# Head 1's first loads on ScalarE's queue, head 0's first key cast on GpSimd, in a fused block-sparse attention and gated MLP kernel

## The chip, the core and the metric

The kernel runs on one core of one Trainium2 chip. The core has four engines that compute: TensorE (PE in the profile, with its weight loads as PEld), VectorE (DVE), ScalarE (ACT) and GpSimd (POOL). SyncE (SP) only issues DMAs here. SP and ACT each have a DMA queue of their own, which the page lists as q1 (SP) and q10 (ACT). The metric is the device time of one launch in microseconds (us). The kernel before was timed three times: the median is 210.89 us, the lowest 209.82, the highest 212.28.

## The reference

Attention over 4 batches, 8 heads, 768 positions, 64 dimensions per head, in fp32, followed by a gated MLP with a spatial mixing step. In short:

```
scores = q @ k.T / sqrt(64)
allowed = |block_i - block_j| <= 1, or block 0 or 23 on either side,
          or block_j among the 3 sampled blocks of block_i    # blocks of 32
attn = softmax(where(allowed, scores, -1e9)) @ v
x = heads side by side                       # [4, 768, 512]
h = relu(x @ w_in)                           # 1024 wide
u, v = halves of h;  v = (v - mean(v)) / sqrt(var(v) + 1e-6)
v = w_spatial @ v + b_spatial                # over the 768 positions
out = (u * v) @ w_out                        # [4, 768, 512]
```

## The kernel before

**Tiling.** Two heads of one batch make a pair, so there are 16 pairs, four to a batch. Keys, queries and values of a pair are loaded as fp32 with the positions over 128 partitions and six chunks per partition (`load`, tiles `st_k`, `st_q`, `st_v`), cast to bf16 (`cast`, tile `nat` for keys and queries, `vv` for values), and transposed so that the head's 64 dimensions lie on partitions (tile `kq`). Under those 64 rows `kq` has 24 more: for the keys the one-hot of the key's block, for the queries a penalty of -300 per block that is not allowed. One matmul with 88 rows thus gives masked scores.

**Slots.** The main loop runs in slots. In each slot TensorE makes a tile of scores in PSUM (L443 in the first batch, L456 later), ScalarE takes the exponential of it into `a_all` (L448, L460), and some slots later TensorE multiplies it by the values (L489, L507). There are two score tiles (tag `sc`), so TensorE can be at most two slots ahead of ScalarE. The first batch takes 36 slots, cut into thirds of the queries so that work can begin before everything is loaded; pair 0, which comes first, is cut by head: slots 0 to 2 are head 0, slots 3 to 5 head 1. Steps of the MLP are dealt out between the slots by tables written by hand (`STEPS`, `AV_AT`, `ROWS`, `when(...)`).

**Order.** The order on every engine is the order of the program text (`manual_schedule`); each engine and each queue takes its instructions strictly in that order and waits where an instruction's input is not there. What is touched here is the start:

- The mask's one-hot and penalty rows are made from `sampled_blocks` (tile `samp`) by GpSimd and VectorE. TensorE turns the penalty into the mask rows of `kq` (L296), and ScalarE copies two of the three results out of PSUM (L222).
- ScalarE first issues the loads of head 0's keys (chunks 0 to 3, then 4 and 5). Then comes a dummy exponential on the tile `tiny` (L163), ahead of which the activation table is loaded, then the cast of head 0's first keys (L136), then the copies out of PSUM, and from then on the exponentials.
- SyncE issues `samp`, head 0's first queries, head 1's keys, head 1's first queries, and then the loads of the other pairs in the order written: keys, first queries of pair 1, values of pair 0, keys of pair 3, keys of pair 2, and so on, later the first weights of the MLP (`w_f`, L229). `st_k` has three buffers: the load of pair 2's keys is the fourth, and takes the buffer of pair 0.
- GpSimd casts head 0's first queries (L138), head 0's last keys, head 1's keys, copies mask rows (L249), casts head 1's first queries, and then the casts of the other pairs and of the weights in the order in which they are loaded.
- TensorE transposes head 0's keys and queries as they are cast (`head`, L303), and VectorE and ScalarE copy them into `kq` (`split0`, L219 and L222). Head 1 follows in `third()`, which runs behind slot 1's scores on TensorE and ahead of slot 2's. Its bank holds both the keys and the first queries.
- The second thirds of the queries of pairs 1, 2 and 3 are transposed in `tr_rest` at slots 12, 15 and 18 (L290), behind their cast on GpSimd.

Of the kernel before, what the change touches and what calls it, by code (L numbers as in the profile page):

```python
# [17 lines left out]
def _listify(ap: bass.AP) -> bass.AP:  # L18
    t = ap.tensor
    if isinstance(t.shape, tuple):  # L20
        t = dataclasses.replace(t, shape=list(t.shape))
        ap = dataclasses.replace(ap, tensor=t)
    return ap
# [3 lines left out]
def kernel(  # L27
# [16 lines left out]
    nc = tc.nc  # L44
# [50 lines left out]
    def dram(src, p, hs=slice(0, 2), cs=slice(0, NCH)):  # L95
        b, g = divmod(p, NG)
        return src[b, 2 * g + hs.start:2 * g + hs.stop].rearrange(
            "h (p c) d -> p h (c d)", c=NCH)[:, :, cs.start * D:cs.stop * D]

    H0, H1, BOTH = slice(0, 1), slice(1, 2), slice(0, 2)  # L100
    ALLC, C01, C03, C45 = slice(0, NCH), slice(0, TC), slice(0, 2 * TC), slice(2 * TC, NCH)
# [3 lines left out]
    def load(p, nm, hs=BOTH, cs=ALLC, eng=nc.sync):  # L105
        if (nm, p) not in st:
            st[nm, p] = work.tile([128, 2, S // 2], FP32, tag="gt" if (nm, p) == ("v", 0) else "st_" + nm,
                                   bufs=1 if (nm, p) == ("v", 0) else 4 if nm == "q" else 3,
                                   name="st_" + nm)
        eng.dma_start(out=st[nm, p][:, hs, cs.start * D:cs.stop * D],  # L110
                      in_=dram(SRC[nm], p, hs, cs))
# [4 lines left out]
    def nat0_view():  # L116
        return nat[0].rearrange("p c h d -> p (c h d)").rearrange("p (h x) -> p h x", h=2)

    def cast(p, nm, eng, hs=BOTH, cs=ALLC):
        if nm == "v":  # L120
            dst = vv[p % NVV][:, hs, cs, 0:D]
        else:
            if p not in nat:
                nat[p] = work.tile([128, 2 * NCH, 2, D], BF16, tag="nat", bufs=4, name="nat")
            c0 = 0 if nm == "k" else NCH
            dst = nat[p][:, c0 + cs.start:c0 + cs.stop].rearrange("p c h d -> p h c d")[:, hs]
        src = st[nm, p].rearrange("p h (c d) -> p h c d", d=D)[:, hs, cs]
        if p == 0 and nm != "v":
            dst = nat0_view()[:, hs, (c0 + cs.start) * D:(c0 + cs.stop) * D]
            if cs is not C45:  # L130
                dst = dst[:, 0].rearrange("p (i t d) -> p t i d", t=2, d=D)
                src = src[:, 0].rearrange("p (t i) d -> p t i d", t=2)
            else:
                dst = dst.rearrange("p h (c d) -> p h c d", d=D)
        if eng is nc.scalar:
            nc.scalar.activation(out=dst, in_=src, func=AF.Copy)  # L136
        else:
            eng.tensor_copy(out=dst, in_=src)  # L138

    samp = const.tile([KR, 2 * NR], I32)  # L140
    load(0,"k",H0,C03,eng=nc.scalar)
    load(0,"k",H0,C45,eng=nc.scalar)
    nc.sync.dma_start(out=samp[MR], in_=_listify(sampled_blocks).bitcast(I32))
    load(0,"q",H0,C03)
    load(0,"k",H1)
    load(0,"q",H1,C03)


    eq = const.tile([KR, NR + 1, NB], FP32)
# [66 lines left out]
    PL, DV = nc.gpsimd, nc.vector  # L216
# [31 lines left out]
        else:  # L248
            eng.tensor_copy(out=kq[MR, hs, cs], in_=src)  # L249

    cast(0, "k", nc.scalar, H0, C03)
    cast(0, "q", PL, H0, C03)
    rows(H1, K_)
    load(1, "k")
# [638 lines left out]
```

## Time and profile before

| what | value |
|---|---|
| median of three runs | 210.89 us (209.82 to 212.28) |
| profiled execution | 210.49 us, of which 208.7 us are the span shown |
| PE busy | 201.2 us (96%) |
| ACT busy | 167.6 us (80%) |
| DVE busy | 132.5 us (63%) |
| POOL busy | 71.2 us (34%) |
| data moved by DMA | 41.82 MB, of which SP's queue 40.91 MB and ACT's queue 0.59 MB |

The span begins with the first instruction that the profiler shows and ends with the last; the profiled execution is 1.79 us longer than its span. A time in a row of the timeline is counted from the start of the span. In a row of the timeline the first number is the start, the second how long it took from the first to the last of the merged instructions, then come the engine, the line, the operation, the tile written and the tile read, the shapes, and how many instructions were merged; in brackets stands the idle time of the engine just before, and what ended it.

### The profile page before, as it was taken

The page shows a single profiled execution, that of the slowest core. Times are in us where ns is not written, and L with a number is a line of the kernel's source. Part 1 is how long each engine was busy: PE and PEld are TensorE (multiplying, and loading weights), DVE is VectorE, ACT ScalarE, POOL GpSimd, SP SyncE. Part 2 cuts the span into 40 slices and gives each one's busy share as a digit, 9 for nine tenths or more (in the row PEclk, how much of TensorE's full clock was granted, in tenths as well). Part 3 has the DMA queues.
Part 4 walks back from the last instruction along what each step waited for, and adds up shares of the span by engine and source line. Part 5 has one row for each costly group of instructions (what it writes and reads, how often), then busy time and mean ns, then how long its engine had stood idle before and what let it go on. Part 6 is the DMA issues. An engine that isn't in the chain of part 4 may idle for free.

```text
span 208.7 us, 5245 instructions
## 1 busy us (share of the span) xinstructions
PE 201.2 (96%) x2107; PEld 127.6 (61%) x2141; DVE 132.5 (63%) x294; ACT 167.6 (80%) x222; POOL 71.2 (34%) x110
## 2 busy tenths in 40 slices
PE   8899999999999999999999999999999999999993
PEld 6588878766666666655565555665556556544441
DVE  6999687878754545484986455376785433567542
ACT  5899899999989989989998888979999787266021
POOL 5588889566573314042065040131020000003000
PEclk9999999999999999999999999999999999999999
DMA  5999999999999999999735597793101324610266
GB/s 140 341 366 347 291 350 222 296 210 298 256 373 220 276 185 315 260 286 342 181 141 113 115 257 171 231 319 86 38 3 21 67 53 85 244 66 0 50 148 254
DMA packets 64139, 41.82 MB, mean 200 GB/s; under 512 B 45172, under 2 KB 58868, under 8 KB 64116
## 3 DMA queue, kind: packets, MB, share of 16 engines
q1 hardware_dynamic: 63540, 40.91, 75.2%
q10 hardware_dynamic: 576, 0.59, 0.9%
q8 instruction: 16, 0.26, 0.5%
q14 instruction: 7, 0.06, 0.1%
HBM read 24.38 MB, written 6.29 MB: 147 GB/s over the span
## 4 chain that ended last, share of the span: by engine, by line
PE 84%; DMA 7%; ACT 2%; issue 2%; SPq 1%; POOL 1%; DVE 1%; ACTq 0%; POOLq 0%
PE ps_moe L581 31%; PE ps L456 22%; PE ps_av L507 12%; PE ps_t L581 8%; PE ps L443 4%; DMA w_f<-in_moe_w_in_dram 4%; PE ps_sc L581 4%; DMA st_k<-in_k_dram 3%; PE ps_av L489 2%; SPq L110 1%; ACT a_all L448 1%; PE ps L290 1%; POOL w_in_t L235 1%; ACT osb L222 0%; PE ps_av L290 0%
## 5 line engine op out<-in xcount | busy, mean ns | idle before, releaser
L460 ACT ACTIVATE a_all<-ps 128x768 bf16<-128x768 f32 x144 | 113.4, 811 | 14.5 <-PE ps L456 8.3
L456 PE MATMUL ps<-kq 88*128 88x384 bf16 x288 | 70.4, 325 | 0.4
L507 PEld LDWEIGHTS <-a_all 128*128 128x128 bf16 x864 | 45.2, 97 | 20.0
L507 PE MATMUL ps_av<-vv,a_all 128*128 128x65 bf16 x864 | 49.8, 193 | 0.0
L456 PEld LDWEIGHTS <-kq 88*128 88x128 bf16 x288 | 27.7, 98 | 29.7
L581 PE MATMUL ps_moe<-w_in_t,xt 128*128 128x512 bf16 x127 | 38.6, 378 | 0.5
L448 ACT ACTIVATE a_all<-ps 128x1024 bf16<-128x1024 f32 x36 | 34.3, 1026 | 2.5 <-PE ps L443 2.0
L581 PE MATMUL ps_moe<-vn,w_spt 128*128 128x512 bf16 x99 | 30.2, 377 | 0.4
L138 POOL CAST nat<-st_k 128x768 bf16<-128x768 f32 (+2 forms) x17 | 13.4, 790 | 43.3 <-DMA st_k<-in_k_dram 41.6
L620 POOL TENSOR_SCALAR std<-mv 128x3 f32<-128x3 f32 (+1 forms) x9 | 2.1, 238 | 60.8 <-DVE mv L617 43.7
L443 PE MATMUL ps<-kq 88*128 88x256 bf16 (+1 forms) x140 | 21.6, 275 | 0.8 <-DVE kq L219 0.3
L653 DVE SCALAR_TENSOR_TENSOR un<-ps_moe,b_col,un 128x512 bf16<-128x512 f32 x18 | 13.4, 747 | 13.5 <-PE ps_moe L581 11.4
L471 DVE RECIPROCAL rc<-ps_av 128x6 f32<-128x6 f32 (+1 forms) x36 | 6.6, 185 | 23.4 <-PE ps_av L507 21.5
L581 PEld LDWEIGHTS <-xt 128*128 128x128 bf16 x192 | 15.5, 98 | 7.6 <-DVE xt L219 0.2
L581 PE MATMUL ps_moe<-w_out_t,gt 128*128 128x512 bf16 x66 | 19.6, 378 | 0.2
L472 DVE TENSOR_TENSOR xn<-ps_av,rc 128x384 bf16<-128x384 f32 (+1 forms) x36 | 18.5, 513 | 1.2
L616 DVE BATCH_NORM_STATS2 stats<-vn 128x6 f32<-128x512 bf16 x24 | 16.4, 684 | 1.3 <-ACT vn L611 0.9
L138 POOL CAST nat<-st_q 128x768 bf16<-128x768 f32 (+2 forms) x21 | 14.7, 705 | 5.9 <-DMA st_q<-in_q_dram 5.8
L219 DVE COPY kq<-tt 64x1536 bf16<-64x1536 bf16 x24 | 14.9, 620 | 1.8 <-DMA tt<-nat 1.5
L443 PEld LDWEIGHTS <-kq 88*128 88x128 bf16 x140 | 12.5, 97 | 4.6 <-DVE kq L219 0.9
L581 PEld LDWEIGHTS <-w_spt 128*128 128x128 bf16 x144 | 11.6, 98 | 5.6
L138 POOL CAST vv<-st_v 128x768 bf16<-128x768 f32 x15 | 13.0, 867 | 4.1 <-DMA st_v<-in_v_dram 2.7
(83 smaller groups left out, 206.1 us busy)
## 6 DMA issues: line engine op xcount, KB each, us to landing
st_v<-in_v_dram SPq DMA_DIRECT2D x16, 384.0 KB, 6.0
st_k<-in_k_dram SPq DMA_DIRECT2D x15, 384.0 KB, 4.6
out_dram<-osb SPq DMA_DIRECT2D x22, 256.0 KB, 2.9
st_q<-in_q_dram SPq DMA_DIRECT2D x12, 384.0 KB, 4.8
ws_f<-in_moe_w_spatial_dram SPq DMA_DIRECT2D x6, 384.0 KB, 9.1
w_f<-in_moe_w_in_dram SPq DMA_DIRECT2D x8, 256.0 KB, 5.9
w_f<-in_moe_w_out_dram SPq DMA_DIRECT2D x4, 256.0 KB, 4.1
st_q<-in_q_dram SPq DMA_DIRECT2D x6, 128.0 KB, 5.9
```

Source lines behind the costliest of these rows:

```text
L138: eng.tensor_copy(out=dst, in_=src)
L219: nc.vector.tensor_copy(out=o, in_=i)
L443: nc.tensor.matmul(out=ps[:, at:at + n * TW], lhsT=kq[:, h, ci * 128:(ci + 1) * 128], rhs=kq[:, h, qcols(t0, n)], start=True, stop=True)
L448: nc.scalar.activation(out=out, in_=ps, func=AF.Exp, scale=0.125)
L456: nc.tensor.matmul(out=ps[:, hf * 512:hf * 512 + HALF], lhsT=kq[:, j % H, ci * 128:(ci + 1) * 128], rhs=kq[:, j % H, S + hf * HALF:S + (hf ...
L460: nc.scalar.activation(out=a_ref["h", j][:, ci, :].rearrange("p (b c) -> p b c", b=2), in_=ps.rearrange("p (b c) -> p b c", b=2)[:, :, 0:H ...
L471: nc.vector.reciprocal(out=rc[:, 0:n], in_=ps[:, :, D:VA])
L472: nc.vector.tensor_tensor(out=out, in0=ps[:, :, 0:D], in1=rc[:, 0:n].to_broadcast([128, n, D]), op=ALU.mult)
L507: nc.tensor.matmul(out=av_ref[j][:, qc, 0:VA], lhsT=a_ref["h", j][:, ci, qc * 128:(qc + 1) * 128], rhs=vv[p % NVV][:, h, ci, 0:VA], start= ...
L581: nc.tensor.matmul(out=ref["ps"][:, 0:w], lhsT=lhs(i), rhs=rhs(i), start=(i == 0), stop=(i == n - 1))
L616: nc.vector.bn_stats(out=stats, in_=self.vn[:, tcc, :])
L653: nc.vector.scalar_tensor_tensor(out=self.un[:, tcc, :], in0=ps, scalar=b_col[:, tcc:tcc + 1], in1=self.un[:, tcc, :], op0=ALU.add, op1=AL ...
```

## The change

Two loads go from SyncE's queue to ScalarE's: all of head 1's keys in pair 0 (192 KB) and head 1's first queries (128 KB). They are issued behind the two loads that ScalarE already issued. And the cast of head 0's first keys, 128 partitions by 256 elements, goes from ScalarE to GpSimd, where it stands ahead of the cast of head 0's first queries.

```diff
     load(0,"k",H0,C03,eng=nc.scalar)
     load(0,"k",H0,C45,eng=nc.scalar)
+    load(0,"k",H1,eng=nc.scalar)
+    load(0,"q",H1,C03,eng=nc.scalar)
     nc.sync.dma_start(out=samp[MR], in_=_listify(sampled_blocks).bitcast(I32))
     load(0,"q",H0,C03)
-    load(0,"k",H1)
-    load(0,"q",H1,C03)
...
-    cast(0, "k", nc.scalar, H0, C03)
+    cast(0, "k", PL, H0, C03)
     cast(0, "q", PL, H0, C03)
     rows(H1, K_)
```

## The prediction

> **What bounds the kernel now.** I read the page first, then the waits of TensorE and ScalarE stretch by stretch, then the first 30 us of the timeline, engine by engine.
>
> ```profile
> PE 201.2 (96%) x2107; PEld 127.6 (61%) x2141; DVE 132.5 (63%) x294; ACT 167.6 (80%) x222; POOL 71.2 (34%) x110
> ```
>
> TensorE is the engine of the whole span, but the edit touches the first microseconds. The question is which engine sets the pace there, and how much of a shift at the start reaches the end. ScalarE's timeline up to 30 us:
>
> ```profile
> 0.72 0.88 ACTq L110 DMA_DIRECT2D st_k<-in_k_dram  x2
> 1.63 1.28 ACT L163 ACT_TABLE_LOAD   x1 [1.63 <-PEq L877]
> 2.93 0.20 ACT L163 ACTIVATE tiny<-tiny 128x1 f32<-128x1 f32 x1
> 3.04 0.40 ACT L136 ACTIVATE nat<-st_k 128x256 bf16<-128x256 f32 x1
> 4.29 0.37 ACT L222 ACTIVATE kq<-mq 24x256 bf16<-24x256 f32 x1 [0.86 <-PE mq L296]
> ...
> 6.03 15.48 ACT L448 ACTIVATE a_all<-ps 128x1024 bf16<-128x1024 f32 x16 [0.57 <-PE ps L443]
> 22.11 5.83 ACT L448 ACTIVATE a_all<-ps 128x1024 bf16<-128x1024 f32 x6 [0.60 <-PE ps L443]
> ```
>
> The reader is to see the two long rows. From 6.03 to 21.51 sixteen exponentials run without a gap, 15.48 / 16 = 0.97 us each. In that stretch ScalarE sets the pace: an input that comes earlier buys nothing, one that comes too late opens a gap. At 21.51 comes the first gap, 0.60 us. TensorE's timeline has the reason, and GpSimd's the reason behind that:
>
> ```profile
> 21.02 0.40 PE L290 MATMUL ps<-ident,nat 128*128 128x128 bf16 x4 [0.43 <-POOL nat L138]
> ```
>
> ```profile
> 3.77 0.40 POOL L138 CAST nat<-st_q 128x256 bf16<-128x256 f32 x1 [0.99 <-DMA st_q<-in_q_dram]
> 4.11 0.29 POOL L138 CAST nat<-st_k 128x128 bf16<-128x128 f32 x1
> 4.79 0.51 POOL L138 CAST nat<-st_k 128x384 bf16<-128x384 f32 x1 [0.39 <-DMA st_k<-in_k_dram]
> 5.36 0.82 POOL L249 COPY kq<-kq 24x768 bf16<-24x768 bf16 x1
> 6.25 0.49 POOL L138 CAST nat<-st_q 128x256 bf16<-128x256 f32 x1
> ...
> 16.82 0.61 POOL L138 CAST nat<-st_q 128x512 bf16<-128x512 f32 x1 [0.47 <-DMA st_q<-in_q_dram]
> 17.49 0.61 POOL L249 COPY kq<-kq 24x512 bf16<-24x512 bf16 x1
> 18.47 0.61 POOL L235 CAST w_in_t<-w_f 128x512 bf16<-128x512 f32 x1 [0.37 <-DMA w_f<-in_moe_w_in_dram]
> 19.03 0.82 POOL L138 CAST vv<-st_v 128x768 bf16<-128x768 f32 x1
> 19.80 0.61 POOL L235 CAST w_in_t<-w_f 128x512 bf16<-128x512 f32 x1
> 20.36 0.61 POOL L138 CAST nat<-st_q 128x512 bf16<-128x512 f32 x1
> ```
>
> The cast of pair 2's later queries, 20.36 to 20.97, ends TensorE's wait. GpSimd comes to it late because it stood 0.47 us at 16.82 and 0.37 us at 18.47 for transfers. So the gap hangs on DMA, through GpSimd. TensorE's waits from 22 us to the end come back as an empty list: from there it runs on its own order. What the change can win is therefore the gap and little more: 0.43 us on TensorE, 0.60 on ScalarE.
>
> Now DMA. The windows of one microsecond (last three numbers: granted clock, DMA share, GB/s) and SyncE's issues:
>
> ```profile
> 3.00:4.00 1.00, 1.00 (x10) 0.75 (x9) 0.85 (x5) 0.43 (x2) 0.23 (x1) 1.00 0.93 297
> 4.00:5.00 1.00, 1.00 (x7) 0.54 (x6) 0.25 (x1) 0.69 (x2) 0.61 (x3) 1.00 0.66 107
> 5.00:6.00 1.00, 0.97 (x10) 0.67 (x8) 0.90 (x3) 0.44 (x2) 0.94 (x2) 1.00 0.80 268
> 6.00:18.00 12.00, 11.10 (x159) 8.83 (x158) 11.21 (x26) 11.70 (x13) 8.55 (x20) 1.00 1.07 360
> ```
>
> ```profile
> 1.21 0.37 SPq L110 DMA_DIRECT2D st_q<-in_q_dram  x1
> 1.64 0.41 SPq L110 DMA_DIRECT2D st_k<-in_k_dram  x1
> 2.09 0.43 SPq L110 DMA_DIRECT2D st_q<-in_q_dram  x1
> 2.57 0.43 SPq L110 DMA_DIRECT2D st_k<-in_k_dram  x1
> 3.05 0.47 SPq L110 DMA_DIRECT2D st_q<-in_q_dram  x1
> ...
> 4.08 1.61 SPq L110 DMA_DIRECT2D st_k<-in_k_dram  x2
> ```
>
> From 6 to 18 us the engines are full at 360 GB/s. Before, there is a hole: 107 GB/s from 4 to 5, 268 from 5 to 6. Pair 0's 640 KB are through, and pair 1's keys, issued only at 2.57, have hardly begun. Against 297, the rate of the microsecond before, the hole is 190 + 29 = 219 KB, at 360 GB/s 0.61 us; against 360 it is 253 + 92 = 345 KB, 0.96 us.
>
> **The change, part by part.**
>
> *Two issues leave SyncE.* The rows at 1.64 and 2.09 go, and what follows comes 2.57 - 1.64 = 0.93 us earlier: pair 1's keys at 1.64, pair 3's keys at 3.15 in place of 4.08. There the lead ends. Pair 2's keys need the buffer that the cast of head 1's keys sets free, and SyncE waits for it:
>
> ```profile
> SPq L110 <- POOL nat L138: 0.5, 1, 0.5
> ```
>
> That cast ends at 4.79 + 0.51 = 5.30. With the lead SyncE stands there 1.4 us in place of 0.5, and pair 2's keys go out at the same time as before. But four transfers, pair 1's keys and queries, pair 0's values, pair 3's keys (384 + 128 + 384 + 384 = 1280 KB), are in flight 0.93 us sooner, enough for 3.6 us at 360 GB/s. So the hole fills, and the full stream that follows is early by the 0.61 to 0.93 us (the issues' lead is the upper bound). I take 0.7, nearer the lower bound, since the microsecond ahead of the hole ran at 297 and not at 360.
>
> *What the lead is worth.* GpSimd's 0.47 us wait at 16.82 goes, since the transfer comes 0.7 earlier; then the wait of 0.37 at 18.47 too, which with 0.7 earlier is still met. The cast at 20.36 thus starts 0.70 us earlier, at 19.66, bounds 0.61 and 0.84 (both waits, all there is). TensorE needed it 0.43 us before it came. Its wait goes, **-0.43 us**, and ScalarE's gap shrinks from 0.60 to 0.17. Late next is nothing on GpSimd's side but TensorE's own order, so the 0.43 stays to the end.
>
> *Two issues more on ScalarE.* One costs 0.88 / 2 = 0.44 us, two 0.88. The table load begins at 2.51 in place of 1.63, ends at 3.79, the dummy exponential at 4.0. The next work, the copy at 4.29, waits for TensorE: 0.29 us of cover are left. Cost 0. If the table load or the issues took longer, each 0.1 us above 0.29 would shift the first exponential by as much; the only table load in the trace is this one of 1.28.
>
> *The cast moves.* On ScalarE it could not stay without cost: it would start at 4.1 in place of 3.04. On GpSimd the nearest rows with 128x256 are 0.40 and 0.49 us. The keys land 2.2 us after their issue at 0.72, so at 2.92; GpSimd is then idle (0.99 us before 3.77). The cast ends at 3.32 to 3.41; now it ends at 3.44.
>
> ```profile
> st_k<-in_k_dram ACTq DMA_DIRECT2D x1, 128.0 KB, 2.2
> 3.86 0.34 PEld L296 LDWEIGHTS <-bm 24*128 24x128 bf16 x3 [0.20 <-DVE bm L187]
> ```
>
> TensorE's next step waits for the mask at 3.86 anyway, so up to 0.1 us earlier buys nothing. Even as long as a 128x768 cast (0.82) it would be done at 3.74, before the queries that GpSimd casts next at 3.77. Cost 0, from 0 to the 0.1 by which a late end would push that cast.
>
> *Head 0's queries in new company.* The first exponential hangs on them: landing 2.5 us after 1.21, cast at 3.77, transposes at 4.61, copy, scores, exponential at 6.03. The rows are that landing, TensorE's weight load for the transposes, and the landing of head 1's keys:
>
> ```profile
> DMA to landing us min/median/max: 2.5/2.5/2.5
> 4.61 0.13 PEld L303 LDWEIGHTS <-nat 128*128 128x128 bf16 x2 [0.41 <-POOL nat L138]
> st_k<-in_k_dram SPq DMA_DIRECT2D x1, 192.0 KB, 3.1
> ```
>
> Head 1's keys are issued at 1.60 on ScalarE in place of 1.64 on SyncE, so the bytes in flight are the same, but they no longer stand behind the queries in one queue. Bounds: 0.3 us earlier (a landing in 2.2, as for the 128 KB above), or 1.03 later (landing with head 1's keys at 1.64 + 3.1 = 4.74). If half the 128 KB goes at half of 297 GB/s, it is 64 / 297 = 0.2 later. I take 0.1, which ScalarE's remaining gap of 0.17 at 21.51 takes up. The Trainium skill, page "DMA: Bandwidth & Descriptors", section "Queues, rings and completion order", says that each DMA engine goes round-robin between the queues that have work; by that rule two queues get half each, and the sum would take the 0.2, which leaves the total within 0.03 us of where it is. No run here shows the shares.
>
> **Sum** against the profiled execution: 210.49 - 0.43 + 0 + 0 + 0 = 210.06 us. The median of the three runs lies 0.40 above that execution; for the median I give **210.5 us**.
>
> **Rivals.**
>
> *The lead is hidden (210.9).* The bytes are the same, and if the hole at 4 to 6 us comes from the transfers' start and not from late issues, it merely moves. For it: 2.2 to 2.5 us pass from an issue to a landing even of the first ones. Against it: pair 0's 640 KB and the hole fit the issue times. Then GpSimd's casts stay where they are: 0. The Trainium skill, same page, section "Issuing engines are not separate DMA queues", states that issuing from several engines saves only the time of the issuing sequencer. By that rule the gain is at most the 0.93 us of SyncE's two issues, and nothing if something else holds the stream.
>
> *Head 1 comes late (slower, 211.7).* Head 1's first queries now land at 2.09 + 3.8 = 5.89 and are cast at 6.25; behind the cast, in TensorE's order, stand slot 2's scores. The rows are the landing of head 1's first queries, those scores, and the landing of pair 1's keys:
>
> ```profile
> DMA to landing us min/median/max: 3.8/3.8/3.8
> 7.11 0.59 PE L443 MATMUL ps<-kq 88*128 88x512 bf16 x2
> DMA to landing us min/median/max: 5.6/5.6/5.6
> ```
>
> Slot 2's exponential starts at 6.03 + 2 x 0.97 = 7.97 and needs scores from 7.38 on; they run at 7.11, so there are 0.27 us, and the cast may start as late as 6.52. That is where this rival decides. If pair 1's keys, now 0.93 us earlier, press the small load back until it lands as those do now (2.57 + 5.6 = 8.17), the cast starts 1.65 us too late and ScalarE's row of sixteen tears. Against it: the load has ScalarE's queue nearly to itself. Between 0 and 1.65 I take half, 0.8: 210.9 + 0.8 = 211.7; upper end 212.5. With head 0's 1.03 on top it would be 213.6.
>
> *More than the gap (210.0).* If ScalarE's next gap (0.29 us at 28.24) closes too, 0.60 + 0.29 = 0.89 off: 210.0.
>
> ```profile
> 28.24 2.14 ACT L448 ACTIVATE a_all<-ps 128x1024 bf16<-128x1024 f32 x2 [0.29 <-PE ps L443]
> ```
>
> **How the numbers follow.** Forecast 0.45, hidden 0.22, head 1 late 0.20, more than the gap 0.08, something that I do not see 0.05. A change of 1%, 2.1 us, is about what a measurement of this kernel can tell from none: its three runs lie 1.07 below to 1.39 above the median. No case but the pile-up of delays reaches 1% by itself; the spread of the runs adds on both sides. Faster by over 1%: 0.05 from forecast and hidden, 0.03 from more than the gap, 0.02 unseen, 0.10. Slower: 0.10 from the upper half of head 1 late, 0.04 from the spread, 0.03 unseen, 0.17. Within 1%: 0.73. The range goes from 210.0 - 1.1 = 208.9 to the late case's upper end and a little of the spread, 212.7.
>
> **What would show it.** Right: pair 1's keys issued near 1.64; the window from 4 to 5 us near 300 GB/s; no wait of GpSimd at 16 to 18.5; the gap at 21.5 under 0.3; first exponential at 6.0 to 6.2. Wrong: the hole still there (hidden); head 1's query cast after 6.5 and a gap among the first sixteen exponentials (late); a copy at 4.29 that follows the dummy exponential without idle time (ScalarE's issues cost more than their cover).

## The result and the profile after

The changed kernel is slower: 212.88 us (median of six runs, 212.49 to 214.43) against 210.64 for the kernel before in the same comparison, a ratio of 1.012 with a 95% interval of 1.0086 to 1.0155. The profiled execution took 212.74 us; its span is 210.6 us, 1.9 more than before. The forecast was 210.5, no change.

The page's first part; the busy time of ScalarE is what it was, TensorE's is 2.2 us more:

```profile
PE 203.4 (97%) x2107; PEld 129.4 (61%) x2141; DVE 135.7 (64%) x294; ACT 167.6 (80%) x221; POOL 72.3 (34%) x111
```

ScalarE's timeline, the same stretch as in the prediction:

```profile
0.72 1.38 ACTq L110 DMA_DIRECT2D st_k<-in_k_dram  x3
2.12 0.49 ACTq L110 DMA_DIRECT2D st_q<-in_q_dram  x1
2.64 1.28 ACT L163 ACT_TABLE_LOAD   x1 [2.64 <-issue]
...
6.45 1.98 ACT L448 ACTIVATE a_all<-ps 128x1024 bf16<-128x1024 f32 x2 [0.99 <-PE ps L443]
9.60 1.02 ACT L448 ACTIVATE a_all<-ps 128x1024 bf16<-128x1024 f32 x1 [1.17 <-PE ps L443]
...
12.20 4.87 ACT L448 ACTIVATE a_all<-ps 128x1024 bf16<-128x1024 f32 x5 [0.26 <-PE ps L443]
17.44 12.37 ACT L448 ACTIVATE a_all<-ps 128x1024 bf16<-128x1024 f32 x13 [0.37 <-PE ps L443]
30.10 2.14 ACT L448 ACTIVATE a_all<-ps 128x1024 bf16<-128x1024 f32 x2 [0.29 <-PE ps L443]
```

The row of sixteen exponentials without a gap is torn. The third one starts at 9.60, where before it would be 6.03 + 2 x 0.97 = 7.97. The tenth starts at 17.44, before at 6.03 + 9 x 0.9675 = 14.74: 2.70 us are lost by then. The 0.60 us gap that stood at 21.51 is gone, and the 23rd exponential starts at 30.10 against 28.24: 1.86 us, about what the span is longer by. GpSimd's timeline shows where it begins:

```profile
2.97 0.40 POOL L138 CAST nat<-st_k 128x256 bf16<-128x256 f32 x1 [0.20 <-DMA st_k<-in_k_dram]
...
6.40 0.51 POOL L138 CAST nat<-st_k 128x384 bf16<-128x384 f32 x1 [2.01 <-DMA st_k<-in_k_dram]
...
7.86 0.40 POOL L138 CAST nat<-st_q 128x256 bf16<-128x256 f32 x1
...
19.43 0.62 POOL L138 CAST nat<-st_q 128x512 bf16<-128x512 f32 x1
```

The moved cast runs at 2.97 and harms nobody. But head 1's keys, the second row, are cast at 6.40, not at 4.79, after 2.01 us of waiting for their DMA. Head 1's queries follow at 7.86, not at 6.25. TensorE meets this in `third()`:

```profile
5.38 1.04 PE L443 MATMUL ps<-kq 88*128 88x256 bf16 x4
...
7.17 0.53 PE L303 MATMUL ps<-ident,nat 128*128 128x128 bf16 x3
8.32 0.40 PE L303 MATMUL ps<-ident,nat 128*128 128x128 bf16 x2 [0.62 <-POOL nat L138]
8.51 1.06 PE L443 MATMUL ps<-kq 88*128 88x512 bf16 x2
```

Slot 2's scores, behind head 1's queries in TensorE's order, run at 8.51 and not at 7.11. VectorE then copies head 1 out of PSUM. Its timeline before, and after:

```profile
6.51 1.97 DVE L219 COPY kq<-ps 64x128 bf16<-64x128 bf16 x6
8.51 1.18 DVE L249 COPY kq<-kq 24x512 bf16<-24x512 bf16 x2
...
10.31 1.41 DVE L219 COPY kq<-ps 64x1024 bf16<-64x1024 bf16 x2
```

```profile
6.56 0.47 DVE L219 COPY kq<-ps 64x128 bf16<-64x128 bf16 x2
8.75 1.36 DVE L219 COPY kq<-ps 64x384 bf16<-64x384 bf16 x4 [1.72 <-PE ps L303]
...
12.62 1.41 DVE L219 COPY kq<-ps 64x1024 bf16<-64x1024 bf16 x2 [0.64 <-PE ps L290]
```

VectorE stands for 1.72 us, and pair 1's copies (64x1024) come 2.31 us later than before. In the windows before, VectorE was busy 11.21 of the 12 us from 6 to 18 and had little slack in which to catch up; after, it is 9.13. But it is not alone in keeping the delay: just ahead of pair 1's copies it stands once more, 0.64 us, for TensorE's transposes. TensorE's timeline shows no wait between 8.32 and 16 us, and up to 12.4 us the score matmuls of one slot take 1.03 to 1.06 us. The windows after:

```profile
3.00:4.00 1.00, 1.00 (x10) 0.78 (x9) 0.86 (x5) 0.99 (x2) 0.65 (x2) 1.00 0.95 177
4.00:5.00 1.00, 1.00 (x7) 0.54 (x6) 0.25 (x1) 0.83 (x3) 0.39 (x2) 1.00 0.96 356
5.00:6.00 1.00, 1.00 (x9) 0.60 (x7) 0.90 (x3) 0.43 (x2) 0.00 (x0) 1.00 1.09 333
6.00:18.00 12.00, 11.12 (x128) 8.62 (x127) 9.13 (x20) 9.40 (x10) 10.40 (x23) 1.00 0.97 326
```

The hole from 4 to 6 us is filled, though from 3 to 4 us less moves than before, 177 GB/s for 297. Whose bytes filled it is in the DMA rows of the first 5 us, by queue (q1 is SyncE's, q10 ScalarE's), first before, then after, with the landings of head 1's keys and queries:

```profile
q1 hardware_dynamic: 475, 0.49, 39.3%
q10 hardware_dynamic: 288, 0.20, 14.7%
```

```profile
q1 hardware_dynamic: 396, 0.45, 34.6%
q10 hardware_dynamic: 411, 0.37, 23.1%
st_k<-in_k_dram ACTq DMA_DIRECT2D x1, 192.0 KB, 4.7
st_q<-in_q_dram ACTq DMA_DIRECT2D x1, 128.0 KB, 5.1
```

Before, SyncE's 0.49 MB are all that head 0's queries and head 1's two loads hold (448 KB, 0.46 MB), with 0.03 MB left for pair 1. After, of head 1's 0.33 MB only about 0.37 - 0.20 = 0.17 have moved by 5 us, while SyncE's queue, less head 0's queries (0.13), has moved 0.32 MB of the loads behind them, which are cast from 8.51 us on. Head 1's keys land 4.7 us after their issue, before 3.1; the queries 5.1, before 3.8.

### The profile page after: what moved, and what is told of

It reads as the page before. It is cut to its first block, busy times and chain, and to the rows that moved or that the text cites. A ratio compares the mean times of both kernels' runs of the same rounds, so it can differ in the third digit from the quotient of the medians.

```text
span 210.6 us, 5244 instructions
## 1 busy us (share of the span) xinstructions
PE 203.4 (97%) x2107; PEld 129.4 (61%) x2141; DVE 135.7 (64%) x294; ACT 167.6 (80%) x221; POOL 72.3 (34%) x111
## 4 chain that ended last, share of the span: by engine, by line
PE 90%; issue 3%; ACT 2%; DVE 2%; POOL 1%; DMA 1%; SPq 0%; ACTq 0%; POOLq 0%
PE ps_moe L581 31%; PE ps L456 23%; PE ps_av L507 12%; PE ps_t L581 8%; PE ps L443 7%; PE ps_sc L581 4%; PE ps_av L489 3%; PE ps L290 1%; ACT a_all L448 1%; DMA st_q<-in_q_dram 1%; DVE kq L219 1%; POOL nat L138 1%; PE ps_av L290 0%; ACT osb L222 0%; ACT a_all L460 0%
## 5 line engine op out<-in xcount | busy, mean ns | idle before, releaser
L456 PEld LDWEIGHTS <-kq 88*128 88x128 bf16 x288 | 27.7, 98 | 29.7
L138 POOL CAST nat<-st_k 128x768 bf16<-128x768 f32 (+3 forms) x18 | 13.7, 759 | 40.3 <-DMA st_k<-in_k_dram 40.2
L443 PE MATMUL ps<-kq 88*128 88x256 bf16 (+1 forms) x140 | 24.0, 297 | 0.6 <-DVE kq L219 0.3
L219 DVE COPY kq<-tt 64x1536 bf16<-64x1536 bf16 x24 | 17.6, 733 | 0.3
L138 POOL CAST nat<-st_q 128x768 bf16<-128x768 f32 (+2 forms) x21 | 15.6, 743 | 5.9 <-DMA st_q<-in_q_dram 5.6
L443 PEld LDWEIGHTS <-kq 88*128 88x128 bf16 x140 | 13.3, 103 | 4.6 <-DVE kq L219 0.8
```

The lines of the kernel that those rows point to most:

```text
L219: nc.vector.tensor_copy(out=o, in_=i)
L443: nc.tensor.matmul(out=ps[:, at:at + n * TW], lhsT=kq[:, h, ci * 128:(ci + 1) * 128], rhs=kq[:, h, qcols(t0, n)], start=True, stop=True)
L456: nc.tensor.matmul(out=ps[:, hf * 512:hf * 512 + HALF], lhsT=kq[:, j % H, ci * 128:(ci + 1) * 128], rhs=kq[:, j % H, S + hf * HALF:S + (hf ...
```

## The experiments

The theory after this reading: pair 1's loads, issued 0.93 us earlier, are served beside head 1's and make them late. The rivals: the cast on GpSimd, a fault of ScalarE's queue as such, SyncE's longer wait for a buffer, and TensorE's clock, because four score matmuls take 1.04 us at 5.38 where they took 0.61. A ratio below is to the kernel before, on the same chip, with its 95% interval.

**The cast alone.**

```diff
-    cast(0, "k", nc.scalar, H0, C03)
+    cast(0, "k", PL, H0, C03)
```

> Only the cast of head 0's first keys moves to GpSimd; all loads stay on the queues of before. If head 1's late loads make the loss, this is the time of before, 210.6 us, within 0.5, with the first exponential at 6.0 to 6.1. If the cast on GpSimd is the cause (it stands ahead of the cast of head 0's queries), 212 to 213.

211.25 us, ratio 1.004 (1.0006 to 1.0075). Head 1's keys were cast behind head 0's without a wait. So the cast isn't the cause; the 0.4% are small, and two kernels below that carry the same cast have 1.0006 and 1.0003. The first exponential came at 6.45, not at 6.0 to 6.1: four score matmuls took 1.03 us here too.

**The loads alone.**

```diff
+    load(0,"k",H1,eng=nc.scalar)
+    load(0,"q",H1,C03,eng=nc.scalar)
...
-    load(0,"k",H1)
-    load(0,"q",H1,C03)
```

> Only the two loads move to ScalarE's queue; the cast of head 0's first keys stays on ScalarE, where it now starts at about 4.0 in place of 3.04, behind the table load. If the late loads make the loss, it is at least that of the change: 212.9, and up to 0.6 more because the first transposes start 1 us later: 212.9 to 213.6. If the cast on GpSimd is the cause: 210.6 to 211.5.

212.47 us, ratio 1.0085 (1.0053 to 1.0116), below the 212.9 to 213.6 that was expected. Head 1's keys were cast at 6.40 as in the change. But this run has a late start of its own: behind the two issues and the table load, ScalarE's cast of head 0's keys starts at 4.03 in place of 3.04, and TensorE waits for it. Behind that, TensorE's five transposes of head 1 run without a wait, as its timeline shows:

```profile
4.49 0.39 PE L303 MATMUL ps<-ident,nat 128*128 128x128 bf16 x2 [0.77 <-ACT nat L136]
...
8.12 0.74 PE L303 MATMUL ps<-ident,nat 128*128 128x128 bf16 x5
```

So the loss comes with moving the two loads, but this run does not show that head 1's lateness makes it. The runs that follow bear on that.

**SyncE held back.** The change, with two loads of 0.6 KB in SyncE's queue where the two loads had been.

```diff
     load(0,"q",H0,C03)
+    for i in range(2):
+        again = const.tile([KR, 2 * NR], I32, name=f"again{i}")
+        nc.sync.dma_start(out=again[MR], in_=_listify(sampled_blocks).bitcast(I32))
```

> The changed kernel, with two small loads (0.6 KB each, the sampled blocks again, into tiles that nothing reads) on SyncE behind head 0's queries, so that pair 1's keys are issued at about 2.6 us again. Theory one, that pair 1's early keys press head 1's loads back: head 1's keys land at 4.7 to 5.2 in place of 6.4 and the time goes back to 210.4 to 211. Theory two, that a third and fourth load on ScalarE's queue are slow by themselves: head 1's keys still land after 6 and the time stays at 212.5 to 213.

211.12 us, ratio 1.0006 (0.998 to 1.0032): the loss is gone, though the time is 0.1 us above the range that was expected. Pair 1's keys go out at 2.86, 0.29 us later than in the kernel before. From the timeline SyncE's issue of pair 1's keys, from the DMA issues the landings of head 1's keys and queries:

```profile
2.86 0.41 SPq L110 DMA_DIRECT2D st_k<-in_k_dram  x1
```

```profile
st_k<-in_k_dram ACTq DMA_DIRECT2D x1, 192.0 KB, 2.7
st_q<-in_q_dram ACTq DMA_DIRECT2D x1, 128.0 KB, 3.9
```

ScalarE's queue carries the same four loads as in the change, and head 1's keys land in 2.7 us in place of 4.7. The queue is not slow; what is issued beside it decides.

**Head 1's loads late without ScalarE's queue.** The kernel before, with the order in SyncE's queue changed.

```diff
-    load(0,"k",H1)
-    load(0,"q",H1,C03)
...
     load(1, "k")
+    load(0,"k",H1)
+    load(0,"q",H1,C03)
     load(1, "q", cs=C01)
```

> The kernel before, with head 1's two loads behind pair 1's keys, all on SyncE's queue: no load is moved to ScalarE, the cast stays on ScalarE. Theory one (head 1's loads are late because pair 1's keys are in flight before or beside them): head 1's keys land after 6 us and the time is 212 to 213.5, as in the change, without ScalarE's queue. Rival (a fault of ScalarE's queue): 210.6 to 211.2.

212.7 us, ratio 1.0072 (1.0035 to 1.0109). The keys were cast at 5.81 and the queries at 7.28, and the kernel lost 0.7%, where the change lost 1.2%. The loss needs neither ScalarE's queue nor the moved cast. Its ten executions are not alike, though: three took 210.63 to 211.11 us, no longer than the kernel before often does, and seven 212.41 to 213.63. What sets the three apart is not shown; only one of the seven was profiled. GpSimd's timeline:

```profile
5.81 0.51 POOL L138 CAST nat<-st_k 128x384 bf16<-128x384 f32 x1 [1.25 <-DMA st_k<-in_k_dram]
7.28 0.40 POOL L138 CAST nat<-st_q 128x256 bf16<-128x256 f32 x1
```

ScalarE's 23rd exponential in the same execution:

```profile
30.34 2.14 ACT L448 ACTIVATE a_all<-ps 128x1024 bf16<-128x1024 f32 x2 [0.29 <-PE ps L443]
```

**One of the two loads.** First only the queries on ScalarE's queue, then only the keys; the other load stays on SyncE ahead of pair 1, and the cast is on GpSimd in both.

```diff
+    load(0,"q",H1,C03,eng=nc.scalar)
...
-    load(0,"q",H1,C03)
```

> Head 1's keys stay on SyncE ahead of pair 1's keys, only head 1's queries go to ScalarE's queue, and the cast is on GpSimd. Theory one: head 1's keys land at 4.7 to 5.2 since they stand ahead of pair 1's keys in the same queue, and the time is 210.2 to 211. Theory two: the queries on ScalarE's queue are late too (landing after 6.5), time 211.5 or more.

```diff
+    load(0,"k",H1,eng=nc.scalar)
...
-    load(0,"k",H1)
```

> Only head 1's keys go to ScalarE's queue; head 1's queries stay on SyncE ahead of pair 1's keys, which are issued at about 2.1 us; cast on GpSimd. Theory one: the keys share with pair 1's keys and land at 5.2 to 6.2, later than the 4.7 of before and earlier than the 6.4 of the change, time 211.2 to 212.4. If only a lead of 0.9 us of pair 1's keys does harm: 4.7 to 5.0 and 210.6 to 211.1.

210.96 us (1.0003, 0.9968 to 1.0038) and 211.1 us (1.0014, 0.9983 to 1.0044). With half the lead (pair 1's keys issued at 2.09 or 2.10, not 2.57) neither loses measurably. GpSimd casts head 1's keys and queries at these times, first of the one kernel, then of the other:

```profile
5.06 0.51 POOL L138 CAST nat<-st_k 128x384 bf16<-128x384 f32 x1 [0.67 <-DMA st_k<-in_k_dram]
6.51 0.41 POOL L138 CAST nat<-st_q 128x256 bf16<-128x256 f32 x1
```

```profile
5.41 0.51 POOL L138 CAST nat<-st_k 128x384 bf16<-128x384 f32 x1 [1.02 <-DMA st_k<-in_k_dram]
6.99 0.40 POOL L138 CAST nat<-st_q 128x256 bf16<-128x256 f32 x1
```

The keys' landing moved to 5.4, inside the 5.2 to 6.2 that was expected, but the time I expected for it, 211.2 to 212.4, was just too high. By casts of the queries the four cases line up: 6.51 and 6.99 cost nothing that can be measured, 7.28 and 7.86 cost 0.7 to 1.2%. With 6.99 the traces already show the late loads: TensorE waited 0.77 us for the cast, and ScalarE's third exponential 1.14.

**The clock.** Both kernels were profiled in a second execution. Below, full rate means that the score matmuls of one slot take about 0.60 us, and half rate that they take about 1.05.

> The kernel before once more, for a second profile. Theory clock by chance of phase: the full rate may come at another time than 5.1 us (up to 9.5), with the span longer by up to 0.6 where it comes later. Late loads: head 1's keys are cast at 4.7 to 4.9 again.

> The changed kernel once more, for a second profile. Theory clock by chance of phase: the moment from which the score matmuls take 0.60 us for four lies elsewhere than 12.5 us. Late loads: head 1's keys are cast at 6.3 to 6.5 again.

The kernel before, TensorE's and ScalarE's timeline in this execution:

```profile
5.38 1.04 PE L443 MATMUL ps<-kq 88*128 88x256 bf16 x4
...
9.03 0.73 PE L443 MATMUL ps<-kq 88*128 88x256 bf16 x4
```

```profile
6.45 1.99 ACT L448 ACTIVATE a_all<-ps 128x1024 bf16<-128x1024 f32 x2 [0.99 <-PE ps L443]
8.79 6.62 ACT L448 ACTIVATE a_all<-ps 128x1024 bf16<-128x1024 f32 x7 [0.36 <-PE ps L443]
...
28.66 3.97 ACT L448 ACTIVATE a_all<-ps 128x1024 bf16<-128x1024 f32 x4 [0.29 <-PE ps L443]
```

The same kernel ran its first scores at half rate and reached the full rate only at about 9.2 us, and still its 23rd exponential came at 28.66, 0.42 us behind the first execution's; this one took 211.26 us. Head 1's keys were cast from about 4.37, earlier than the 4.7 to 4.9 that was expected. The slow first scores are thus no mark of the change. Against this execution, which starts at the same rate, the change's third exponential is 0.81 us late, its tenth 1.56 and its 23rd 1.44. The changed kernel took 213.26 in its second execution, cast head 1's keys at 6.56, a little later than expected, and was at half rate until about 12.5 again, so that its moment did not lie elsewhere, as the clock theory had it. Its 23rd exponential started at 30.38.

> The changed kernel, with the three transposes of head 1's keys made three times over in the same place (six more matmuls into columns that get the same values), so that TensorE is busy where it now waits for head 1's queries. Theory clock: in the change's profile the score matmuls run at half rate until 12.5 us (1.05 us for four in place of 0.60) because TensorE's wait before 8.3 us leaves a window too idle; busy, they are at full rate from about 9.3 at the latest, and the time is 0.3 to 0.9 below the change: 212.0 to 212.6. Theory late loads alone: the rate does not depend on that wait, time 212.7 to 213.1.

```diff
-        head(ps1, 1, 0, NCH)
+        for _ in range(3):
+            head(ps1, 1, 0, NCH)
```

212.45 us (five runs), ratio 1.0094 (1.0059 to 1.0129). That lies in the range that the clock theory gave, 212.0 to 212.6, but the interval overlaps the change's: by time it decides nothing. Its profile says more. There the rate was full from the first scores, the queries were cast at 7.61, the third exponential still waited 1.04 us, and the 23rd started at 29.70, 1.46 us behind the kernel before at full rate:

```profile
5.19 0.61 PE L444 MATMUL ps<-kq 88*128 88x256 bf16 x4 [0.15 <-DVE kq L219]
```

```profile
8.82 1.02 ACT L449 ACTIVATE a_all<-ps 128x1024 bf16<-128x1024 f32 x1 [1.04 <-PE ps L444]
```

> The kernel before, with three more filler matmuls ahead of the transposes of head 0's queries, where TensorE waits 0.41 us, and one more behind them. Theory clock: the full rate comes by 6 us in more of the runs, the median falls by 0.1 to 0.6 to 210.3 to 210.8. Theory late loads alone: the clock at the start is no part of the loss and of no use here, 210.9; if the filler delays the transposes, 211.0 to 211.3.

```diff
-    FILL, FILL2, FILL3 = 24, 4, 4
+    FILL, FILL2, FILL3 = 24, 5, 4
...
+    filler(3, wps)
     psq = bank("psq", "av")
```

211.12 us, ratio 1.0024 (0.9997 to 1.005): no gain, although its profile has the full rate from 5.05. So work on the rate at the start bought nothing that shows.

**SyncE's wait for the buffer.** The change with a fourth buffer for the keys; then the kernel with only the queries moved, with the same buffer.

```diff
-                                   bufs=... else 4 if nm == "q" else 3,
+                                   bufs=... else 4 if nm in "qk" else 3,
...
-    lim = const.tile([KR, NCH, 128], BF16)
+    lim = kq[MR, 1, K_].rearrange("b (c p) -> b c p", c=NCH)
...
```

> The changed kernel with a fourth buffer for the loaded keys, so that the load of pair 2's keys no longer waits for the cast of head 1's keys (room for it by keeping the mask's limits in rows that head 1's keys take later). If the loss is TensorE's and ScalarE's wait for head 1 alone: 212.4 to 213.0, as the change, though SyncE no longer stands from 3.8 to 6.9. If a part of the loss is SyncE's long wait and the hole in DMA at 8 to 12 us that follows it: 211.2 to 212.2.

> Only head 1's queries on ScalarE's queue, the cast on GpSimd, and the fourth buffer for the loaded keys: a try at a kernel faster than both. If SyncE's wait for the buffer costs anything here: 210.0 to 210.7. If not, 210.8 to 211.2; if more transfers in flight press head 1's queries back, 211.3 to 212.

212.7 us, ratio 1.0094 (1.0065 to 1.0123), and 210.84 us, ratio 0.9993 (0.9963 to 1.0024). In the first, SyncE issued pair 2's keys by 4.3 us where the change had stood until 6.9, and the loss stayed. The windows from 8 to 10 and 10 to 12 us moved 352 and 358 GB/s, where the change had 283 and 246: the hole in DMA behind that wait is not the cause. This execution ran at full rate as well, so ScalarE's timeline shows the late loads without the half rate:

```profile
8.46 1.02 ACT L448 ACTIVATE a_all<-ps 128x1024 bf16<-128x1024 f32 x1 [0.50 <-PE ps L443]
...
29.27 3.05 ACT L448 ACTIVATE a_all<-ps 128x1024 bf16<-128x1024 f32 x3 [0.29 <-PE ps L443]
```

With the keys cast at 5.79 and the queries at 7.25, the 23rd exponential starts 29.27 - 28.24 = 1.03 us late. The second kernel was a try at beating both; it equals the kernel before. None was found that beats it.

## Why the prediction was wrong

**What bounds the kernel now: right, with one omission.** ScalarE did set the pace, and "one that comes too late opens a gap" is what happened. What I did not read in the windows that I quoted is VectorE's 11.21 of 12 us: behind a wait there, little can be caught up.

**Two issues leave SyncE: right, but for the end of the wait.** Pair 1's keys went out at 1.65, pair 3's at 3.34, and SyncE stood for head 1's cast. Since that cast came late itself, pair 2's keys went out at 6.94, not at the same time as before (5.32). The stream came early: 283 + 177 + 356 + 333 = 1149 KB from 2 to 6 us, against 259 + 297 + 107 + 268 = 931 before, so 218 KB more, where I had worked out a hole of 219. That the two are so close is luck in part: from 4 to 6 us it was 314 KB more, and from 3 to 4 us 120 less.

**What the lead is worth: not shown, and the sign of the sum wrong.** The cast of pair 2's later queries started at 19.43, not 20.36, and TensorE's wait and ScalarE's gap went. But in the second execution of the kernel before, without any lead, the same cast started earlier still, and neither the wait nor the gap was there:

```profile
19.15 0.61 POOL L138 CAST nat<-st_q 128x512 bf16<-128x512 f32 x1
```

So the 0.43 us, the only term of the sum that was not 0, was a wait of one execution, and no run shows that it went because of the lead. Nor does the 2.70 - 1.86 = 0.84 us that the change won back by its 23rd exponential make a gain: it lies under a larger loss.

**Two issues more on ScalarE, the cast moves: right.** Table load to 3.92, the copy still at 4.29; the cast at 2.97 in 0.40 us. Cost 0 shows in the held-back kernel, which has both and 1.0006.

**Head 0's queries in new company: right.** Landing in 2.4 us against 2.5. The first exponential at 6.45 is the half rate, which the kernel before had too in its second execution.

**The step that failed** is that the sum had no term for head 1's loads. I put them among the rivals at 0.20, since "the load has ScalarE's queue nearly to itself". That sentence is the error. A queue of one's own isn't bandwidth of one's own: what protected head 1's loads before was that they stood in SyncE's queue ahead of pair 1's. The change took them from there and in the same stroke sent 1280 KB out 0.6 to 0.9 us sooner (pair 1's keys at 1.65 for 2.57, pair 0's values at 2.93 for 3.56). The bytes that I counted as filling the hole are the ones that pressed them back; I had both numbers and let the same transfers be early in one step and harmless in the next. The rival's mechanism and place were right: head 1's keys took 4.7 us to land in place of 3.1, and 2.7 where SyncE was held back. Its point of decision, a cast of the queries at 6.52, is not settled. 6.51 cost nothing, and from 7.28 on there is a loss; at 6.99 its rule asks for 0.47 us, and the interval there, -0.4 to 0.9 us, holds both that and no loss.

Its price was too low: with the cast at 7.86 its own rule gives 1.34 us, 212.2; measured were 2.24 in the medians. Part of what it left out shows at full rate. There the 23rd exponential came 1.03 us late with the cast at 7.25 (fourth buffer) and 1.46 late with it at 7.61 (TensorE kept busy), 0.30 and 0.37 more than the rule gives; in both, VectorE's timeline shows no idle time between its last copies of head 1 and 15 us in which to catch up. TensorE's rate is likely another part. With the cast at 7.28, but at half rate behind the wait, the kernel with the changed order in SyncE's queue came 30.34 - 28.24 = 2.10 us late. Those two kernels differ in more than the rate, so the 1.07 us between them are no clean price of it. How much of the 2.24 the half rate adds stays open.

The Trainium skill's sentence that I cited for the hidden lead (page "DMA: Bandwidth & Descriptors", section "Issuing engines are not separate DMA queues") says that the transfers of all issuers run on the same engines and interleave. The trace agrees, with 0.17 MB of head 1 and 0.32 MB of others moved by 5 us. I drew from it only that nothing is won, and not that head 1's loads would be mixed with the others.

## What to carry to other kernels

When a load is taken out of a queue, ask what moves up into its place, and whether the load now has to compete with it: here the order within one queue had protected the urgent load, and the second queue gave that up. Where DMA is busy, something not urgent that is issued earlier can be paid for by whatever is urgent at that time, so price the urgent load first. Look behind the wait for engines with no slack (here VectorE, 93% busy, and TensorE at half rate): with them a wait stays. And do not build a forecast on a gap seen in one execution: a second profile of the kernel before would have shown that the 0.43 us come and go.

## What the runs showed of the hardware that I had not expected

**The granted clock in the windows does not show a start at half rate, but shows a fall to it.** It reads 1.00 in every window above, while four score matmuls took 1.04 us in one execution of the kernel before and 0.61 in another, at the same 5.38 us. The Trainium skill, page "TensorE: Matmul & The Clock Gate", section "Part 1: The HAM clock gate (the 'warmup' mystery)", says that the array starts at half rate and goes to the full rate after a busy window of about 3.4 us, which runs freely and does not begin with the kernel; the two executions of one kernel agree with that, at full rate by 5.38 us in one and from about 9.2 in the other.

When the wait for head 1 is long the rate can fall back. With only the keys moved, TensorE's timeline shows full rate ahead of a wait of 0.77 us and half rate behind it, while the change with four buffers kept the full rate through one of 0.79. Here the granted clock, the third number from the end, does tell it:

```profile
5.91 0.60 PE L443 MATMUL ps<-kq 88*128 88x256 bf16 x4 [0.23 <-DVE kq L219]
...
7.45 0.40 PE L303 MATMUL ps<-ident,nat 128*128 128x128 bf16 x2 [0.77 <-POOL nat L138]
7.63 1.06 PE L443 MATMUL ps<-kq 88*128 88x512 bf16 x2
```

```profile
7.00:8.00 1.00, 0.56 (x3) 0.35 (x4) 0.12 (x1) 0.60 (x1) 1.00 (x9) 0.72 1.01 318
8.00:9.00 1.00, 1.00 (x7) 0.55 (x6) 0.92 (x4) 0.27 (x1) 0.80 (x2) 0.50 1.03 382
```

In the kernel with the changed order in SyncE's queue, behind a wait of 1.01 us, it reads 0.50 from 8 to 14 us. The wait that a late load makes can thus cost TensorE its rate as well.
